# Batch 2's score products all raw in the prologue and tile 1, squares summed by adding DMAs, softmax chain in a fixed order

## The chip, the cores and the metric

The kernel runs on one core of one Trainium2 chip. The metric is the device time of one execution in microseconds; for the kernel before it is the median of two runs.

## The reference

Four batches of a channel attention, then a feed-forward layer on its output:

```python
B, N, C = (4, 6080, 256)
qn = q / (np.linalg.norm(q, axis=1, keepdims=True) + 1e-06)
kn = k / (np.linalg.norm(k, axis=1, keepdims=True) + 1e-06)
s = kn.transpose(0, 2, 1) @ qn / tau
a = softmax(s)                        # over the last axis, 256 x 256 a batch
x = (v @ a).reshape(B * N, C)         # 24320 x 256
h = x @ w_in                          # 256 x 2048
out = np.maximum(0.01 * h, h) @ w_out # 2048 x 256
```

The softmax line stands for four lines of the reference (maximum off, exponential, sum, division). The scores need, besides the product of k and q over 6080 rows, the sum of squares of each column of q and of k.

## The kernel before, in words

**Tiles and windows.** The output is made in 24 tiles (6 a batch, `NT`), each of 1024 rows (the last of a batch 960), in two halves. A tile has 8 windows (`NPAIR`), one for each pair of 128-wide slices of the 2048 hidden channels, twice over; so a batch has 48 windows (`WPB`). The loop at L854 to L894 issues one window after another. In a window, seven `block_product` calls (L546) of three matmuls each form a Strassen-like product of a split `v` and the combined weights `w_split`; ACT copies the sums (`taken`, L574), DVE adds (`add`, L569), ACT applies the leaky function and casts, DVE forms the low part (`leaky`, L557). The matmuls with `w_out` (`ffn_out`, L583) of the window before are dealt out between them by `out(n)`, 24 a window. All float32 values of these products are kept as a high and a low part in float32r, and a product takes three passes.

**Weights of a batch.** The combined weights are `w_in` multiplied by the batch's turned softmax matrix `aT`: `w_product` (L395) on PE, `w_taken` (L409) on ACT, `w_parts` (L417) on DVE, which gives six steps for each of four `j`: two of sums (L430, L431), then for each of two pairs `begin` (three blocks split) and `rest` (four blocks). For batch 1, `w_parts` writes straight into `w_split` tiles (`w_tile`, L390: 4 buffers) that the windows of tile 1 use; for `j` 1 to 3 it runs inside tile 1 (`w_early`, L698). From tile 2 on, `w_load` (L481) fetches them from DRAM.

**Scores.** Class `Scores` (L110). The 6080 rows are 48 chunks of 128 (one with 64 rows), in 24 groups of `G` = 2. `load` (L124) fetches a group of q and k with two DMAs from SP. `product(j)` (L168) multiplies a chunk either raw, as float32 (two calls), or, where `cast` (ACT, L157) and `low` (DVE, L162) have made a split tile, in six float32r calls. `square` (ACT, L151) and `add_square` (DVE, L154) sum the squares of a chunk. Then comes the softmax chain: `sums`, `norms_mm` (PE), `norms_taken`, `norms_begun`, `norms` (DVE), `rows_mm` (PE), `rows_taken`, `scaled` (DVE), `exps` (ACT), `normed` (DVE), `turn` (PE), `turned_high` (ACT), `turned_low` (DVE).

**The prologue** (L767 to L842) does batch 1's 24 groups raw (squares in whole groups, added by DVE at L142), its softmax chain, the split of tile 1's `v` (`v_parts`, L520, eleven steps on DVE), the first `w_product` and `w_parts`, and between them `FILL` = 5 groups, 10 chunks, of batch 2, raw. The order of instructions on an engine is chosen there by the framework's scheduler, by the order of the program and its own estimates, save where `tc.issue_after` sets a lower limit. Raw groups of batch 2, conversion blocks and weights share the tag `raw` (4 buffers).

**Conversions.** `w_in` and `w_out` arrive as 64-bit floats; `f64_split` (L320) turns a block into two parts with work on DVE and ACT. Four of 16 blocks are done in the prologue's first part, 12 in windows 0 to 5, two a window (`convert`, L741).

**What sets the order in the windows.** `in_order(engine)` (L99) chains an instruction to the last one issued on its engine, so the order of the windows' own work is written out by hand. Background work stands in queues (`todo`, L615); `put(queue, length, fn, then)` (L630) adds an entry with a planned length, and `slot(queue, room)` (L621) at fixed places of a window takes entries from the head of that queue while they fit in the room. `at(w, fn)` (L618) sets the window in which an entry is put. Batch 2's remaining 38 chunks are put by `chunk_work` (L652) in windows 8 to 33 (L752 to L758): cast and square on ACT, low part and add on DVE, the six matmuls in the next window. Its softmax chain is put from window 34 on (`norm_work`, `row_work`, `turn_work`, L664 to L677), and the weights for tile 7 (`w_work`, L679) from window 39. Batches 3 and 4 do all 48 chunks split.

SP issues all DMAs, in one queue, POOL a memset for the short chunk of each batch.

## Time and profile before

| | |
|---|---|
| median of 2 runs | 2224.7 us (2224.56 to 2224.85) |
| span of the profiled execution, first to last instruction | 2225.9 us |
| mean granted clock of TensorE | 0.990 |
| busy PE / weight load | 2174.0 us / 1814.1 us |
| busy DVE / ACT / POOL | 1488.5 us / 1483.2 us / 2.8 us |
| DMA | 324.74 MB, mean 146 GB/s |

PE is TensorE's matmul, PEld its weight load, DVE VectorE, ACT ScalarE, POOL GpSimd, SP SyncE. The profiled execution's span lies 1.2 us above the median of the runs. Times in views are microseconds from the start of the span, unless ns is written; a wait is written as the waiting instruction, an arrow, and what released it, with the total, the number of waits and the longest. The granted clock is the share of full speed that the throttle let through. L12 is line 12 of the kernel. The end of a matmul is modelled; the distance from one start to the next is what shows its cost.

### The profile page before, as it was taken

What the parts mean: (1) busy time and instruction counts of PE and PEld (TensorE: products, weight loads), DVE (VectorE), ACT (ScalarE), POOL (GpSimd) and SP (SyncE); (2) the same over time, 40 slices, a digit from 0 to 9 for tenths busy, and PEclk for the clock granted to TensorE, in tenths of its full rate; (3) what the DMA queues carried; (4) which work ended last, traced back from release to release, by engine and by line L of the source; (5) the groups of instructions that cost most, each with busy time, mean ns of one, the idle gap of its engine ahead of it and who ended that gap; (6) DMA issues with size and microseconds to landing.
All of it is one profiled execution on the core that took longest, in us unless ns stands there. A gap on an engine that the chain in (4) does not pass through costs nothing.

```text
span 2225.9 us, 27253 instructions
## 1 busy us (share of the span) xinstructions
PE 2174.0 (98%) x9940; PEld 1814.1 (81%) x9940; DVE 1488.5 (67%) x2651; ACT 1483.2 (67%) x2563; POOL 2.8 (0%) x10
## 2 busy tenths in 40 slices
PE   9679999999999999999999999999999999999999
PEld 7467888888888888888887888888888888888887
DVE  7986667666766776666766667676677655556554
ACT  6556777766657777776656777777665666666665
POOL 0000000000000000000000000000000000000000
PEclk9889999999999999999999999999999999999999
DMA  9435343342753434433464344343354432332331
GB/s 347 145 142 200 121 155 134 130 157 83 241 204 112 156 123 145 154 116 138 147 227 156 119 159 159 115 155 129 121 192 156 146 137 83 138 121 100 119 118 36
DMA packets 98967, 324.74 MB, mean 146 GB/s; under 512 B 10257, under 2 KB 22033, under 8 KB 98833
## 3 DMA queue, kind: packets, MB, share of 16 engines
q1 hardware_dynamic: 98832, 323.00, 42.1%
q8 instruction: 78, 1.28, 0.2%
q14 instruction: 57, 0.46, 0.1%
HBM read 264.50 MB, written 58.46 MB: 145 GB/s over the span
## 4 chain that ended last, share of the span: by engine, by line
PE 89%; DVE 5%; DMA 3%; ACT 2%; issue 0%; SPq 0%; ACTq 0%; DVEq 0%
PE ps_o L597 44%; PE ps_x L551 22%; PE ps_z L551 11%; PE ps_y L551 5%; PE ps_s L182 5%; PE ps_s L401 1%; DMA qk_raw<-in_k_dram 1%; DVE h L572 1%; DVE g_split L565 1%; DMA w_dram<-w_rest 1%; ACT h L562 1%; ACT g_split L563 1%; DMA f_raw<-in_w_out_dram 1%; DMA qk_raw<-in_q_dram 1%; DVE v_split L516 0%
## 5 line engine op out<-in xcount | busy, mean ns | idle before, releaser
L597 PE MATMUL ps_o<-g_split,w_out_split 128*128 128x512 f32 (+1 forms) x4608 | 1165.5, 388 | 0.0
L597 PEld LDWEIGHTS ps_o<-g_split,w_out_split 128*128 128x128 f32 x4608 | 867.7, 188 | 175.5
L565 DVE TENSOR_TENSOR g_split<-h,g_split 128x512 fp32r<-128x512 f32 (+1 forms) x768 | 525.0, 684 | 395.3 <-ACT g_split L563 394.4
L551 PE MATMUL ps_x<-v_split,w_split 128*128 128x512 f32 (+1 forms) x2304 | 653.7, 392 | 29.4 <-DVE w_split L439 16.2
L562 ACT ACTIVATE h<-h 128x512 f32<-128x512 f32 (+1 forms) x576 | 361.8, 628 | 292.3 <-DVE h L572 292.3
L578 ACT COPY h<-ps_x 128x512 f32<-128x512 f32 (+1 forms) x576 | 334.3, 580 | 312.4 <-PE ps_x L551 311.7
L551 PEld LDWEIGHTS ps_x<-v_split,w_split 128*128 128x128 f32 x2304 | 423.7, 189 | 114.0 <-ACT h L578 12.4
L563 ACT CAST g_split<-h 128x512 fp32r<-128x512 f32 (+1 forms) x768 | 473.4, 616 | 23.9
L572 DVE TENSOR_TENSOR h<-ps_z,h 128x512 f32<-128x512 f32 (+1 forms) x384 | 262.0, 682 | 284.7 <-ACT h L578 278.0
L551 PE MATMUL ps_z<-v_split,w_split 128*128 128x512 f32 (+1 forms) x1152 | 324.4, 390 | 6.3 <-DVE h L572 6.3
L551 PEld LDWEIGHTS ps_z<-v_split,w_split 128*128 128x128 f32 x1152 | 216.5, 188 | 52.5 <-DVE h L572 8.1
L551 PE MATMUL ps_y<-v_split,w_split 128*128 128x512 f32 (+1 forms) x576 | 162.9, 391 | 0.6 <-ACT w_a L411 0.6
L572 DVE TENSOR_TENSOR h<-ps_y,h 128x512 f32<-128x512 f32 (+1 forms) x192 | 131.3, 684 | 0.6
L551 PEld LDWEIGHTS ps_y<-v_split,w_split 128*128 128x128 f32 x576 | 109.0, 190 | 23.5 <-ACT w_a L411 1.1
L182 PEld LDWEIGHTS ps_s<-qk_split 128*128 128x128 f32 x804 | 114.1, 190 | 11.3 <-issue 1.0
L562 ACT ACTIVATE h<-ps_x 128x512 f32<-128x512 f32 (+1 forms) x192 | 112.8, 587 | 10.8 <-PE ps_x L551 10.8
L182 PE MATMUL ps_s<-qk_split 128*128 128x256 f32 x804 | 118.1, 283 | 0.0
L160 ACT CAST qk_split<-qk_raw 128x512 fp32r<-128x512 f32 x134 | 82.9, 619 | 31.8 <-PE ps_s L182 24.0
L516 DVE TENSOR_TENSOR v_split<-v_raw,v_split 128x512 fp32r<-128x512 f32 (+1 forms) x144 | 98.7, 686 | 4.7
L155 DVE TENSOR_TENSOR sq_acc<-sq_acc,sq 128x512 f32<-128x512 f32 x141 | 96.2, 683 | 0.0
L164 DVE TENSOR_TENSOR qk_split<-qk_raw,qk_split 128x512 fp32r<-128x512 f32 x134 | 91.6, 684 | 2.3 <-ACT qk_split L160 2.3
L152 ACT ACTIVATE sq<-qk_raw 128x512 f32<-128x512 f32 x141 | 88.8, 633 | 2.0 <-DMA qk_raw<-in_k_dram 2.0
(101 smaller groups left out, 726.7 us busy)
## 6 DMA issues: line engine op xcount, KB each, us to landing
w_split<-w_dram SPq DMA_DIRECT2D x184, 896.0 KB, 4.7
qk_raw<-in_q_dram SPq DMA_DIRECT2D x92, 256.0 KB, 3.6
qk_raw<-in_k_dram SPq DMA_DIRECT2D x92, 256.0 KB, 3.8
v_raw<-in_vT_dram SPq DMA_DIRECT2D x40, 512.0 KB, 4.9
out_dram<-o_sb SPq DMA_DIRECT2D x80, 256.0 KB, 4.2
win<-win_dram SPq DMA_DIRECT2D x24, 512.0 KB, 4.1
w_dram<-w_rest SPq DMA_DIRECT2D x24, 512.0 KB, 3.1
w_dram<-w_first SPq DMA_DIRECT2D x24, 384.0 KB, 3.4
```

The lines of the kernel that those rows point to most:

```text
L152: return nc.scalar.activation(out=out, in_=self.chunk(j), func=AF.Square)
L155: return nc.vector.tensor_tensor(out=self.acc[0], in0=self.acc[0], in1=sq, op=ALU.add)
L164: return nc.vector.tensor_tensor(out=sp[:, :, 1, :], in0=self.chunk(j), in1=f32(sp[:, :, 0, :]), op=ALU.subtract)
L182: mm = nc.tensor.matmul(out=s, lhsT=lhsT, rhs=rhs, start=False, stop=last and n == len(passes) - 1, skip_group_check=True,)
L516: last = nc.vector.tensor_tensor(out=sp[:, 1, 0:w], in0=src, in1=f32(sp[:, 0, 0:w]), op=ALU.subtract)
L551: mm = nc.tensor.matmul(out=ps[:, 0:n], lhsT=w[:, x, a, :], rhs=sp[:, y, 0:n], start=first and k == 0, stop=k == 2, skip_group_check=True,)
L562: nc.scalar.activation(out=out[:, 0:n], in_=h[:, 0:n], func=AF.Prelu, alpha=0.01)
L563: issued["act"] = nc.scalar.copy(out=sp[:, 0, 0:n], in_=out[:, 0:n])
L565: issued["dve"] = nc.vector.tensor_tensor(out=sp[:, 1, 0:n], in0=out[:, 0:n], in1=f32(sp[:, 0, 0:n]), op=ALU.subtract)
L572: issued["dve"] = nc.vector.tensor_tensor(out=h[:, 0:n], in0=ps[:, 0:n], in1=h[:, 0:n], op=ALU.add)
L578: issued["act"] = nc.scalar.copy(out=h[:, 0:n], in_=ps[:, 0:n])
L597: issued["pe"] = nc.tensor.matmul(out=o_ps[i][j][h][:, 0:n], lhsT=wo[x][:, f, h * P:(h + 1) * P], rhs=sp[:, y, 0:n], start=p == 0 and earl ...
```

## The change

- The prologue multiplies 8 groups (16 chunks) of batch 2 raw instead of 5, loaded into buffers of `g_split` (groups 0 to 4) and `w_split` (groups 5 to 7) by `spare`. The engines' order from `sums` on is written out by `run`, which chains each step to the one before it on its engine; steps of `v_parts` stand between those of the chain, and the weight steps are issued in the order 2, 0, 1, 3, then three of `v`, then 4, 5.
- The other 16 groups are put raw into windows 0 to 7, two a window (`group_work`): four entries in queue `pe`, squares of a whole group in `act`. Their raw tiles use the tag `qk_split` (3 buffers); a group is loaded for at the window before its own.
- Squares: group 0's go straight into the accumulator (a tile in the buffer of `w_rest`), each other group's are written over its raw tile, and a DMA from POOL adds that tile into the accumulator. `fold` adds the two halves on DVE after the last. The tile of raw data is free when its adding DMA is done.
- Batch 2's softmax chain starts at window 12 instead of 34, its steps 4 windows apart instead of 2; the weights for tile 7 start at window 21 instead of 39.
- The high part of tile 1's `v` is copied by ACT, and in tile 1 one slot of ACT has room for 2.2 instead of 1.8.

The diff (left out: `sums` now returns its last instruction):

```diff
--- before.py
+++ after.py
@@ -21,7 +21,7 @@
 AHEAD = 8
 EARLY_LOAD = (12, 14, 16, 18)
 EARLY_SPLIT = (17, 19, 21, 23)
-FILL = 5
+FILL = 8
 VBUFS = 10
 GBUFS = 5
 RBUFS = 4
@@ -143,6 +143,20 @@
 
         def first_squares(self, i):
             nc.scalar.activation(out=self.acc[i], in_=self.raw[i], func=AF.Square)
+
+        def group_product_squares(self, i):
+
+            raw = self.raw[i]
+            if i == 0:
+                return nc.scalar.activation(out=self.acc[0], in_=raw, func=AF.Square)
+            ins = nc.scalar.activation(out=raw, in_=raw, func=AF.Square)
+            nc.gpsimd.dma_start(out=self.acc[0], in_=raw, accum_op=ALU.add)
+            return ins
+
+        def fold(self, acc):
+            both = self.acc[0]
+            self.acc = [acc]
+            return nc.vector.tensor_tensor(out=acc, in0=both[:, :, 0, :], in1=both[:, :, 1, :], op=ALU.add)
 
         def chunk(self, j):
             i, x = self.of[j]
...
@@ -512,7 +529,7 @@
     def v_split_of(i, name, src):
         w = widths[i % NT]
         sp = work.tile([P, 2, TW], F32R, name="v_split", tag="v_split", bufs=VBUFS)
-        nc.vector.tensor_copy(out=sp[:, 0, 0:w], in_=src)
+        (nc.scalar.copy if i == 0 else nc.vector.tensor_copy)(out=sp[:, 0, 0:w], in_=src)
         last = nc.vector.tensor_tensor(out=sp[:, 1, 0:w], in0=src, in1=f32(sp[:, 0, 0:w]), op=ALU.subtract)
         v_split[i, name] = sp
         return last
@@ -661,6 +678,13 @@
             sq = temp(name="sq").rearrange("p (x c) -> p x c", x=2)
             put("act", 0.6, lambda: sc.square(j, sq), [("dve", 0.7, lambda: sc.add_square(sq))])
 
+    def group_work(sc, i):
+
+        a, b = sc.groups[i]
+        put("pe", 0.5, lambda: sc.product(a))
+        then = [("dve", 0.7, lambda: sc.fold(acc_tile()))] if i == len(sc.groups) - 1 else []
+        put("pe", 0.5, lambda: sc.product(b), [("act", 1.05, lambda: sc.group_product_squares(i), then)])
+
     def norm_work(sc):
         put("pe_late", 1, sc.norms_mm, [
             ("dve", 0.5, sc.norms_taken, [("dve", 1.8, sc.norms_begun, [("dve", 2.0, sc.norms)], True)], True),
@@ -749,19 +773,27 @@
     for b in range(1, B):
         w0 = (b - 1) * WPB
         sc = scores[b]
-        done = FILL * G if b == 1 else 0
-        begin_at, span = (NPAIR, 25) if b == 1 else (2, 31)
-        when = {j: w0 + begin_at + (j - done) * span // (NCHUNK - done) for j in range(done, NCHUNK)}
-        for i in range(done // G, len(sc.groups)):
-            at(max(w0, when[i * G] - 3), lambda sc=sc, i=i: sc.load(i, qk_raw()))
-        for j in range(done, NCHUNK):
-            at(when[j], chunk_work, sc, j)
-        e = w0 + begin_at + span + 1
+        if b == 1:
+            per = -(-(len(sc.groups) - FILL) // NPAIR)
+            for i in range(FILL, len(sc.groups)):
+                w = w0 + (i - FILL) // per
+                at(max(w0, w - 1), lambda sc=sc, i=i: sc.load(i, work.tile([P, 2, G, C], F32, name="qk_raw1", tag="qk_split", bufs=3)))
+                at(w, group_work, sc, i)
+            e = w0 + NPAIR + 4
+        else:
+            begin_at, span = 2, 31
+            when = {j: w0 + begin_at + j * span // NCHUNK for j in range(NCHUNK)}
+            for i in range(len(sc.groups)):
+                at(max(w0, when[i * G] - 3), lambda sc=sc, i=i: sc.load(i, qk_raw()))
+            for j in range(NCHUNK):
+                at(when[j], chunk_work, sc, j)
+            e = w0 + begin_at + span + 1
+        apart = 4 if b == 1 else 2
         at(e, norm_work, sc)
-        at(e + 2, row_work, sc)
-        at(e + 4, turn_work, sc)
-        at(e + 1, win_load, 0)
-        at(e + 5, w_work, b, 0)
+        at(e + apart, row_work, sc)
+        at(e + 2 * apart, turn_work, sc)
+        at(e + 2 * apart - 3, win_load, 0)
+        at(e + 2 * apart + 1, w_work, b, 0)
 
 
     sc, nxt = scores[0], scores[1]
@@ -794,52 +826,70 @@
             sc.product(j)
         if i in EARLY_SPLIT:
             conv.split()
-    sc.sums()
-    sc.norms_mm()
-    sc.norms_taken()
-    sc.norms_begun()
-    after["dve"] = sc.norms()
+
+    def run(engine, fn, *args):
+        with in_order(engine):
+            issued[engine] = ins = fn(*args)
+        return ins
+
+    def spare(i):
+        if i < GBUFS:
+            return work.tile([P, 2, G, C], F32, name="qk_raw1", tag="g_split", bufs=GBUFS)
+        t = work.tile([P, 2, NS, P], F32, name="qk_raw1", tag="w_split", bufs=4)
+        return t.rearrange("p x s f -> p (x s f)")[:, 0:2 * G * C].rearrange("p (x g c) -> p x g c", x=2, g=G)
+
+    nxt.begin([work.tile([P, 2, G, C], F32, name="sq_acc1", tag="w_rest", bufs=1)], bank("s"))
+
+    def fill(n):
+        for i in range(n, n + 1):
+            for j in nxt.groups[i]:
+                run("pe", nxt.product, j)
+            run("act", nxt.group_product_squares, i)
+
     with tc.issue_after(after["load"].ins):
-        for i in range(min(2, FILL)):
-            nxt.load(i, qk_raw())
-    sc.rows_mm()
-    sc.rows_taken()
-    after["scaled"] = sc.scaled()
-    sc.exps()
-    after["normed"] = sc.normed()
-    nxt.begin([acc_tile()], bank("s"))
-    filled = []
-
-    def fill(n):
-        for i in range(len(filled), min(len(filled) + n, FILL)):
-            for j in nxt.groups[i]:
-                nxt.product(j)
-                if j == 0:
-                    nxt.square(j, nxt.acc[0])
-                else:
-                    sq = temp(name="sq").rearrange("p (x c) -> p x c", x=2)
-                    nxt.square(j, sq)
-                    nxt.add_square(sq)
-            if i + 2 < FILL:
-                nxt.load(i + 2, qk_raw())
-            filled.append(i)
-
-    with tc.issue_after(after["dve"].ins):
-        fill(2)
-    sc.turn("x")
-    sc.turned_high()
-    after["turned"] = sc.turned_low()
-    with tc.issue_after(after["scaled"].ins):
-        fill(1)
-        for _, fn in v_parts(0):
-            fn()
+        for i in range(FILL):
+            nxt.load(i, spare(i))
+    v_tile = [fn for _, fn in v_parts(0)]
+
+    def v_do(n):
+        for fn in v_tile[:n]:
+            run("dve", fn)
+        del v_tile[:n]
+
+    fill(0)
+    run("dve", sc.sums)
+    run("pe", sc.norms_mm)
+    fill(1)
+    fill(2)
+    run("dve", sc.norms_taken)
+    run("dve", sc.norms_begun)
+    run("dve", sc.norms)
+    run("pe", sc.rows_mm)
+    fill(3)
+    fill(4)
+    v_do(1)
+    run("dve", sc.rows_taken)
+    run("dve", sc.scaled)
+    run("act", sc.exps)
+    fill(5)
+    v_do(2)
+    run("dve", sc.normed)
+    run("pe", sc.turn, "x")
+    fill(6)
+    run("act", sc.turned_high)
+    v_do(2)
+    run("dve", sc.turned_low)
     for h in range(CH):
-        w_product(0, 0, h, "yz"[h])
-        w_taken(0, 0, h)
-    for _, fn in w_parts(0, 0):
-        fn()
-    with tc.issue_after(after["turned"].ins):
-        fill(FILL)
+        run("pe", w_product, 0, 0, h, "yz"[h])
+        run("act", w_taken, 0, 0, h)
+    fill(7)
+    v_do(3)
+    order = list(w_parts(0, 0))
+    for x in (2, 0, 1, 3):
+        run("dve", order[x][1])
+    v_do(3)
+    for x in (4, 5):
+        run("dve", order[x][1])
 
     outs = []
 
@@ -872,7 +922,7 @@
             slot("dve", 2.2)
             block_product(i, p, x, S2, "T2", False, False)
             h12 = taken(i, x)
-            slot("act", 1.8)
+            slot("act", 1.8 if i else 2.2)
             block_product(i, p, z, S1, "T1", True, False)
             out(5)
             slot("pe", 1)
```

More of the change, by code (lines that the diff above doesn't have):

```diff
@@ L192, in sums @@
             nc.vector.tensor_tensor(out=acc, in0=acc, in1=other, op=ALU.add)
-            nc.vector.tensor_tensor(out=acc[:, :, 0, :], in0=acc[:, :, 0, :], in1=acc[:, :, 1, :], op=ALU.add)
+            last = nc.vector.tensor_tensor(
+                out=acc[:, :, 0, :], in0=acc[:, :, 0, :], in1=acc[:, :, 1, :], op=ALU.add
+            )
             self.acc = [acc[:, :, 0, :]]
+            return last
         def norms_mm(self):
```

## The prediction

> **What bounds the kernel now.** I read the page of the profile first, then a table of busy times by stretch, cut where the windows of tile 1 begin, then who waited for whom on PE.
>
> ```profile
> span 2225.9 us, 27253 instructions
> PE 2174.0 (98%) x9940; PEld 1814.1 (81%) x9940; DVE 1488.5 (67%) x2651; ACT 1483.2 (67%) x2563; POOL 2.8 (0%) x10
> PE   9679999999999999999999999999999999999999
> ```
>
> PE is the bound from the fourth slice on. Only the second and third slices have room on it.
>
> ```profile
> 48.70:77.50 28.80, 17.72 (x71) 13.47 (x71) 26.91 (x67) 12.65 (x25) 0.00 (x0) 0.86 0.54 191
> 77.50:92.70 15.20, 10.78 (x28) 7.09 (x28) 12.90 (x33) 5.44 (x10) 0.00 (x0) 0.59 0.50 190
> 92.70:112.70 20.00, 12.75 (x51) 9.26 (x52) 17.22 (x35) 14.84 (x26) 0.00 (x0) 0.94 0.36 121
> 112.70:127.30 14.60, 14.13 (x51) 10.89 (x52) 12.52 (x32) 7.33 (x14) 0.00 (x0) 0.85 0.44 177
> 127.30:146.10 18.80, 12.32 (x52) 9.23 (x50) 13.80 (x28) 12.61 (x22) 0.00 (x0) 0.96 0.32 112
> 146.10:164.90 18.80, 15.54 (x52) 11.90 (x52) 16.58 (x38) 8.37 (x15) 0.00 (x0) 0.77 0.41 155
> 164.90:180.20 15.30, 12.41 (x53) 9.30 (x51) 11.27 (x23) 10.15 (x18) 0.00 (x0) 1.00 0.47 134
> 180.20:192.20 12.00, 10.69 (x46) 8.42 (x47) 7.87 (x22) 5.65 (x10) 0.00 (x0) 1.00 0.83 319
> 192.20:202.40 10.20, 10.20 (x47) 8.45 (x46) 8.73 (x16) 6.48 (x12) 0.00 (x0) 1.00 0.25 89
> 202.40:500.00 297.60, 297.60 (x1418) 250.38 (x1417) 202.78 (x327) 216.64 (x376) 0.00 (x0) 1.00 0.42 145
> ```
>
> The columns are the stretch, its length, the busy time of PE, weight load, DVE, ACT and POOL, the granted clock, the DMA share and GB/s. The first row is the softmax chain of batch 1, the next eight are windows 0 to 7 (tile 1), the last is windows 8 to about 34, in which batch 2's other 38 chunks are multiplied. Three readings. In the last row PE is busy 297.6 of 297.6 us: work taken off PE there shortens the run one for one. Tile 1 takes 124.9 us, and PE is busy in 98.8 of them, some at a clock of 0.59 to 0.85: there is room, 26.1 us and more. Window 7, with neither conversions nor new weights, takes 10.2 us, all PE.
>
> ```profile
> PE ps_x L551 <- DVE w_split L439: 16.2, 4, 5.3
> PE ps_x L551 <- ACT h L578: 7.2, 7, 1.9
> PE ps_x L551 <- DVE w_split L440: 5.0, 3, 3.0
> ```
>
> In tile 1, PE waits above all for the next pair's weights from DVE, four times and up to 5.3 us. DVE is busy 12.5 to 17.2 us in windows 1 to 4, near the whole length: tile 1 is a chain through DVE.
>
> **Term 1, products taken out of windows 8 to 34.** What a chunk costs on PE, split and raw, is read from starts.
>
> ```profile
> 49.63 3.62 PE L182 MATMUL ps_s<-qk_raw 128*128 128x256 f32 x16
> 53.09 0.95 PE L200 MATMUL ps_y<-ones,sq_acc 128*128 128x1 f32 x8
> ...
> 77.47 0.77 PE L551 MATMUL ps_x<-v_split,w_split 128*128 128x512 f32 x1 [3.93 <-DVE w_split L439]
> ...
> 215.08 0.88 PE L182 MATMUL ps_s<-qk_split 128*128 128x256 f32 x6
> 215.79 0.86 PE L551 MATMUL ps_x<-v_split,w_split 128*128 128x512 f32 x3
> L182 PE MATMUL ps_s<-qk_split x228: 277/283/283, 215.1 to 490.3; 128*128 128x256 f32 x114
> ```
>
> (The last row is the group of split products in windows 8 to 34.) A split chunk takes 215.79 - 215.08 = 0.71 us; the group's 228 matmuls are 38 chunks of 6. All 38 leave a stretch where PE is full: 38 x 0.71 = **-27.0 us**. The ACT squares and casts and DVE adds and low parts that go with them lay beside that full PE and bring nothing there (cover: PE's 297.6 us). A raw chunk takes 4 recorded matmuls; 16 of them go from 49.63 to 53.09, 3.46 us, so 0.865 us a chunk: raw is dearer on PE by 0.155 us. The 32 chunks put into tile 1 are 27.7 us of PE there; the 6 further ones in the prologue 5.2 us.
>
> **Term 2, the softmax chain.** Rows of DVE's timeline, then ACT's, then the DVE group of the adds that go.
>
> ```profile
> 64.34 0.16 DVE L285 TENSOR_SCALAR den<-den 128x2 f32<-128x2 f32 x1
> 66.34 0.61 DVE L288 TENSOR_SCALAR s_sb<-s_sb,den 128x256 f32<-128x256 f32 x2
> 70.68 0.68 DVE L309 TENSOR_TENSOR aT<-ps_x,aT 128x512 fp32r<-128x512 f32 x1
> 77.10 0.36 DVE L439 CAST w_split<-w_a 128x128 fp32r<-128x128 f32 x2
> ```
>
> ```profile
> 67.95 0.58 ACT L306 CAST aT<-ps_x 128x512 fp32r<-128x512 f32 x1
> 73.59 0.59 ACT L411 COPY w_a<-ps_z 128x512 f32<-128x512 f32 x1
> ```
>
> ```profile
> L155 DVE TENSOR_TENSOR sq_acc<-sq_acc,sq 128x512 f32<-128x512 f32 x9 | 6.2, 684 | 0.0
> L141 ACT ACTIVATE sq<-qk_raw 128x1024 f32<-128x1024 f32 x22 | 23.1, 1054 | 5.5 <-DMA qk_raw<-in_k_dram 5.3
> ```
>
> DVE is busy 26.9 of 28.8 us here, and the chain stands behind other DVE work three times: the normalising waits from 64.50 to 66.34 (1.8 us), the low part of the turned matrix from 68.53 to 70.68 (2.2), the first weights from 74.18 to 77.10 (2.9). A fixed order can give at most these 7 us. Nine adds leave DVE (6.2 us), one v copy goes to ACT. Against it, on PE 16 chunks instead of 10 stand in a fixed order between the steps, and on ACT two squares (2 x 1.05 us) stand ahead of the exponentials and one ahead of the cast of the turned matrix. I give back 3 of the 7: **-4 us**. Bounds: -7 (nothing given back) and +5 (no gain, and the 5.2 us of extra products all on the chain).
>
> **Term 3, 32 raw chunks in tile 1.** Lower bound: each stretch is as long as before or as PE's work, whichever is more, with 4 chunks (3.46 us) a window. Window 0: 10.8 + 3.5 is under 15.2. Windows 1 and 2: 26.9 + 6.9 = 33.8, under 34.6. 3 and 4: 27.9 + 6.9 = 34.8, under 37.6. 5 and 6: 23.1 + 6.9 = 30.0 over 27.3, +2.7. Window 7: +3.5. Sum +6.2. Upper bound: all 27.7, for the products stand ahead of the new pair's weight product in PE's queue, so weights, wait and next window could all move back by their length. Between: in windows 1 and 3 I lose half (3.5 of 6.9), since DVE works off conversions meanwhile, in 0, 2 and 4 a third (3.3 of 10.4), in 5 to 7 the 6.2: **+13 us**. ACT's 16 squares (16.9 us) fit: ACT is busy 70.9 of 124.9 us, and they stand where PE has over 4 us of products before it needs ACT again (T1, 5 out products, two raw chunks, T3).
>
> **Term 4, the adding DMAs.** None exists in this trace: POOL has 10 instructions. Nearest rows (KB each, median us from issue to landing):
>
> ```profile
> qk_raw<-in_k_dram SPq DMA_DIRECT2D x92, 256.0 KB, 3.8
> v_raw<-in_vT_dram SPq DMA_DIRECT2D x40, 512.0 KB, 4.9
> w_dram<-w_rest SPq DMA_DIRECT2D x24, 512.0 KB, 3.1
> qk_raw<-in_q_dram SPq DMA_DIRECT2D x4, 64.0 KB, 2.2
> ```
>
> An add moves 512 KB but reads two operands. Below: one pass, 3.1 us. Above: two of the slowest passes, 9.8 us. From the rows: fixed part 2.2, one pass 3.1 - 2.2 = 0.9, two passes 1.8, with about 0.5 for the issue: T = 4.5 us, nearest to the 512 KB rows. The 23 adds go into one accumulator, so each waits for the last one: they are a chain. It starts when group 1 is squared: norms product 53.09, end about 53.9, products 1.73, square 1.05, say 57. Two places wait for it. (a) Groups 5 to 7 of the prologue lie in three of the four weight buffers; the second pair's weights (the fifth weight step on DVE) need the buffer of group 5, so add 5 done: 57 + 5T. In the new order that step comes at about 80 (weights from 73, then 3.8 of weight steps and 3.3 of v). Queued behind it on DVE: the first adds and low parts of window 0, and for those waits PE. (b) In tile 1 the raw groups share three buffers: group 11 needs group 8's, so add 8 done and a load (3.8): 57 + 8T + 3.8, wanted at about 95 in window 1. Its load waits at the head of SP's queue:
>
> ```profile
> 137.97 9.82 SPq L317 DMA_DIRECT2D f_raw<-in_w_out_dram x4
> ```
>
> behind it there stand loads of raw weights like these, the weight stores and v. At T = 4.5, (a) is 79.5, in time, and (b) 96.8, late by 1.8: **+2 us**. Later groups have 16 to 17 us a pair against 9. The fold on DVE in window 8 waits for the last add, but PE has its last blocks and out products meanwhile: 0. At T = 3.1 the term is 0; at 6.5 it is 9.5 + 8.3 = 17.8; at 9.8 it is 26 + 18, and with 19.6 us a pair against 17 some 14 more, 58.
>
> The Trainium skill (SBUF — State Buffer, Who interferes with whom) speaks against the change: a DMA issued from GpSimd has its descriptors written by GpSimd, which is locked out while VectorE runs a copy, cast or scalar operation in a two-port mode; its example goes from about 620 to 3100 ns. By it an add here would be an estimated 2.5 us longer, 7 us, and the kernel would come out a few us slower than before; by the row above (POOL all but unused) no run here shows it yet, though DVE is 86 to 93% busy in the prologue, windows 1 and 4.
>
> **Sum.** -27 - 4 + 13 + 2 = -16 us. The span is 2225.9 us, 1.2 above the median of 2224.7; the difference taken off the median gives 2208.7, **2209 us**.
>
> **Rivals.**
> *The adds are slow.* Without term 4 the change is worth 18 us, so from T = 6.5 it is lost and from there the kernel is slower. At T = 8: (a) 17, (b) 12.8, together 30, so +12, 2237. At 9.8: +40, 2265. For: no row shows a second operand, other traffic holds the DMA engines at shares of 0.32 to 0.83, and it is one chain. Against: 512 KB passes take 3.1 us, and over tile 1 the chain needs far less than is there.
> *Nothing overlaps.* Term 3 is 27.7: -27 - 4 + 27.7 + 2 = -1.3, 2223. For: the waits for weights end in DVE work that begins after the weight product. Against: PE is idle at other places too (7.2 us for ACT).
> *All overlaps.* Terms 2 and 3 at their good ends, no wait for adds: -27 - 7 + 6.2 = -27.8, 2197. For: slow clocks in tile 1 go away with idle PE. Against: DVE is the chain there and is not relieved.
> *The order isn't what it says:* the fixed order lengthens the chain instead: +5 in term 2, -7 in all, 2218.
>
> **How the numbers follow.** Chances: forecast 0.40 (own range 2201 to 2217), slow adds 0.22, nothing overlaps 0.15, all overlaps 0.18, order costs 0.05. From 2193 to 2240 I leave out half of the slow adds and a little below 2197. 2% is 44 us, about what a measurement of this kernel can tell from no change: a gain of 44 has no term that could bring it (0.02); a loss of 44 needs adds at or above 9.8 us (0.05); within, 0.93.
>
> **What would show it.** Windows 8 to 34 without score products, each 10.2 us and full. Window 0's first product about 4 us earlier. Tile 1 about 138 us instead of 124.9, the granted clock there nearer 1. Adds on a queue of POOL's, some 4.5 us apart while they queue. Wrong: adds of 6.5 us or more, a DVE wait of several us at L439 in window 0, PE waiting for a raw load in window 1, conversions late behind SP, or tile 1 over 150 us.

## The result and the profile after

The changed kernel takes **2262.1 us** (median of 2 runs, 2259.89 to 2264.29) against 2224.7: 37.4 us longer, ratio 1.017 (95% 1.014 to 1.0199). The forecast of 2209 us has the wrong sign, and the time lies 22 us above the upper end of its range. The rival of the slow adds gives such a time for adds between 8 us (2237) and 9.8 us (2265); whether its mechanism is the right one is the question of the experiments.

First the page of the changed kernel: its span, PE's busy time, and PE and the DMA engines in 40 slices.

```profile
span 2258.1 us, 27056 instructions
PE 2180.1 (97%) x9864; PEld 1816.0 (80%) x9864; DVE 1436.8 (64%) x2560; ACT 1463.8 (65%) x2508; POOL 22.9 (1%) x33
PE   7687699999999999999999999999999999999999
DMA  9777723554324434344276343343354432332331
```

PE now has room in five slices instead of two, up to about 280 us, and just there the DMA engines are busy at 0.7 and more.

The table of busy times by stretch, cut as before where a window's first product begins: windows 0 and 1, then 6 to 9, then what follows. The columns are the stretch, its length, PE, weight load, DVE, ACT and POOL busy, granted clock, DMA share, GB/s.

```profile
88.50:110.70 22.20, 12.54 (x46) 9.66 (x44) 10.95 (x29) 6.73 (x11) 2.69 (x3) 0.77 0.85 222
110.70:136.30 25.60, 16.22 (x69) 12.26 (x68) 17.18 (x34) 16.70 (x28) 2.59 (x3) 0.95 0.73 192
...
217.50:233.00 15.50, 15.50 (x61) 12.66 (x62) 7.83 (x22) 7.63 (x12) 0.86 (x1) 0.89 0.91 282
233.00:261.40 28.40, 16.61 (x62) 13.35 (x61) 8.81 (x16) 8.47 (x14) 2.59 (x3) 0.76 0.63 162
261.40:271.60 10.20, 10.20 (x46) 8.45 (x45) 3.65 (x6) 7.86 (x14) 0.86 (x1) 1.00 0.94 283
271.60:289.50 17.90, 12.14 (x46) 9.60 (x45) 7.40 (x12) 6.96 (x13) 0.00 (x0) 0.81 0.42 118
289.50:500.00 210.50, 210.36 (x934) 173.22 (x934) 138.02 (x273) 132.55 (x230) 0.52 (x1) 1.00 0.45 153
```

Three things are to be seen. Window 0's first product runs at 88.5, 11.0 us later than before (77.47), where the forecast had it 4 earlier. Tile 1 takes 172.9 us (88.5 to 261.4) instead of 124.9, where the forecast had 138; the worst window is the last, 28.4 us with 16.6 of PE work, and it has neither conversions nor new weights. And window 9, after the tile, takes 17.9 us for 12.1 of PE work, where the forecast put the wait of the fold at nothing. Behind that PE is full at a clock of 1.00, as forecast. Window 8 starts at 261.4 against 202.4 before: 59.0 us lost (11.0 and 48.0), and 7.7 more in window 9; what follows gives 34.5 back, which leaves the 32.2 us between the two spans.

Who PE waited for, in the whole run (total, times, longest):

```profile
PE ps_x L568 <- ACT h L595: 17.6, 3, 9.7
PE ps_s L196 <- DMA qk_raw<-in_k_dram: 16.9, 4, 11.8
...
PE ps_s L187 <- DMA qk_raw<-in_k_dram: 12.4, 1, 12.4
```

None of them names an adding DMA. The waits of PE name the last step only; one has to ask what that step waited for. The chain of work, followed back through tile 1, does it: 58.4% of the stretch from 88 to 292 us is `DMA sq_acc<-qk_raw`, the adds. Some of its pieces (start, length, what):

```profile
105.86 5.25 DMA sq_acc<-qk_raw
...
146.91 4.60 DMA sq_acc<-qk_raw
...
226.25 11.17 DMA sq_acc<-qk_raw
...
268.76 7.50 DMA sq_acc<-qk_raw
276.28 0.04 DVE sq_acc L159
```

The shortest of all its 23 adds takes 4.5 us, the longest 11.2. The three places where something waits for an add can be read from the timelines, DVE's and PE's here. An engine's idle time and its releaser stand in brackets.

```profile
100.22 0.43 DVE L456 CAST w_split<-w_a 128x128 fp32r<-128x128 f32 x2 [6.78 <-DMA sq_acc<-qk_raw]
276.28 0.69 DVE L159 TENSOR_TENSOR sq_acc<-sq_acc 128x512 f32<-128x512 f32 x1 [6.50 <-DMA sq_acc<-qk_raw]
```

```profile
61.96 2.04 PE L187 MATMUL ps_s<-qk_raw,zeros 128*128 128x512 f32 x2 [12.40 <-DMA qk_raw<-in_k_dram]
104.73 1.65 PE L568 MATMUL ps_x<-v_split,w_split 128*128 128x512 f32 x3 [9.65 <-ACT h L595]
205.79 3.35 PE L196 MATMUL ps_s<-qk_raw 128*128 128x256 f32 x8 [2.87 <-DMA qk_raw<-in_k_dram]
247.45 2.90 PE L196 MATMUL ps_s<-qk_raw 128*128 128x256 f32 x6 [11.79 <-DMA qk_raw<-in_k_dram]
280.03 1.65 PE L568 MATMUL ps_x<-v_split,w_split 128*128 128x512 f32 x3 [5.76 <-ACT h L595]
```

At 100.22 the first weight step of the second pair has waited 6.8 us for the add that still reads its buffer (the forecast's place (a)); the adds of window 0 stand behind it on DVE, so ACT's `h` is late and PE idle for 9.65 us. At 276.28 the fold has waited 6.5 us at the head of DVE's queue, and DVE's adds of window 9 stand behind it: PE idle for 5.76. At 247.45 PE waits for group 22's raw data, whose buffer group 19's add held until 237.4 (226.25 and 11.17); the load itself, beside the next add, takes the other 10 us. The wait at 61.96 has nothing to do with adds: group 0 of the prologue came late. SP's timeline tells why:

```profile
43.35 0.33 SPq L134 DMA_DIRECT2D qk_raw<-in_q_dram  x1
...
49.30 0.38 SPq L334 DMA_DIRECT2D f_raw<-in_w_out_dram  x1
...
52.70 0.48 SPq L129 DMA_DIRECT2D qk_raw<-in_q_dram  x1
...
55.89 0.34 SPq L134 DMA_DIRECT2D qk_raw<-in_k_dram  x1
```

The loads are issued in an order that the program didn't fix: groups 5 to 7 go out from 43.35 on, then conversion blocks (L334), and group 0, the one that the first product needs, only from 52.70 to 55.89 (L129 and L134). The page of the profile gives no order to look for; the line numbers and the start times do.

### The profile page after: what moved, and what is told of

It is laid out like the page before. It is cut to its first block, busy times and chain, and to the rows that moved or that the text cites. A ratio compares the mean times of both kernels' runs of the same rounds, so it can differ in the third digit from the quotient of the medians.

```text
span 2258.1 us, 27056 instructions
## 1 busy us (share of the span) xinstructions
PE 2180.1 (97%) x9864; PEld 1816.0 (80%) x9864; DVE 1436.8 (64%) x2560; ACT 1463.8 (65%) x2508; POOL 22.9 (1%) x33
## 3 DMA queue, kind: packets, MB, share of 16 engines
q1 hardware_dynamic: 98832, 323.00, 41.7%
## 4 chain that ended last, share of the span: by engine, by line
PE 85%; DMA 6%; issue 2%; DVE 1%; ACT 1%; POOLq 0%; SPq 0%; DVEq 0%
PE ps_o L614 43%; PE ps_x L568 21%; PE ps_z L568 11%; PE ps_y L568 5%; DMA sq_acc<-qk_raw 5%; PE ps_s L196 3%; PE ps_s L418 1%; DVE h L589 0%; ACT h L579 0%; ACT g_split L580 0%; DVE g_split L582 0%; DMA w_dram<-w_rest 0%; DMA qk_raw<-in_k_dram 0%; DVE v_split L533 0%; DVE w_rest L457 0%
## 5 line engine op out<-in xcount | busy, mean ns | idle before, releaser
L196 PEld LDWEIGHTS ps_s<-qk_split 128*128 128x128 f32 x576 | 81.7, 190 | 8.3 <-issue 1.0
L196 PE MATMUL ps_s<-qk_split 128*128 128x256 f32 x576 | 84.9, 283 | 0.0
L174 ACT CAST qk_split<-qk_raw 128x512 fp32r<-128x512 f32 x96 | 59.4, 619 | 25.9 <-PE ps_s L196 22.1
L178 DVE TENSOR_TENSOR qk_split<-qk_raw,qk_split 128x512 fp32r<-128x512 f32 x96 | 65.7, 684 | 2.3 <-ACT qk_split L174 2.3
L532 DVE CAST v_split<-v_raw 128x512 fp32r<-128x512 f32 (+1 forms) x138 | 57.4, 416 | 14.1 <-PE ps_x L568 14.1
L196 PE MATMUL ps_s<-qk_raw 128*128 128x256 f32 x192 | 50.1, 411 | 16.9 <-DMA qk_raw<-in_k_dram 16.9
```

The costliest lines, as they stand in the source:

```text
L174: return nc.scalar.copy(out=sp[:, :, 0, :], in_=self.chunk(j))
L178: return nc.vector.tensor_tensor(out=sp[:, :, 1, :], in0=self.chunk(j), in1=f32(sp[:, :, 0, :]), op=ALU.subtract)
L196: mm = nc.tensor.matmul(out=s, lhsT=lhsT, rhs=rhs, start=False, stop=last and n == len(passes) - 1, skip_group_check=True,)
L532: (nc.scalar.copy if i == 0 else nc.vector.tensor_copy)(out=sp[:, 0, 0:w], in_=src)
```

## The experiments

Each edit is against the changed kernel, and its time stands beside runs of the kernel before on the same chip (medians 2223.4 to 2224.7). The question that they share is which effect of the adds costs the time: that they are there at all (traffic), that they hold buffers, or that something stands behind them in a queue.

**Group 0 in time.** The prologue's eight loads are issued in the order 0 to 7, by chaining them, the conversion blocks and tile 1's raw loads on SP's queue (the last two are left out of the cut).

```diff
...
-            nxt.load(i, spare(i))
+            run("sp", nxt.load, i, spare(i))
```

> The changed kernel with one thing added: on SP the eight groups of the prologue are loaded in the order 0 to 7, and the conversion blocks and tile 1's raw groups only after them. Theory (most of the loss is waits for DMAs that were ordered behind others): PE's wait of 12.4 us for group 0 goes, the softmax chain starts about 12 us earlier, the waits for adds stay; 2262 - 12 = 2250 us. Rival (the DMA engines are simply full, at a share of 1.0, and what is loaded later is missed later): conversions come late instead, 2257 us or more.

Measured 2253.8 us, ratio 1.0137 (1.012 to 1.0154): 8.3 us less than the changed kernel. Window 0 starts at 78.6 instead of 88.5, but part of that is lost to the adds again, which begin earlier and stand among more loads. The adds' issues on POOL, and DVE's wait in window 0:

```profile
57.62 1.01 POOL L153 DMA_DIRECT2D sq_acc<-qk_raw  x1 [13.17 <-DMA win_dram<-win_early]
67.11 0.91 POOL L153 DMA_DIRECT2D sq_acc<-qk_raw  x1 [8.49 <-DMA sq_acc<-qk_raw]
76.19 0.86 POOL L153 DMA_DIRECT2D sq_acc<-qk_raw  x1 [8.17 <-DMA f_raw<-in_w_in_dram]
```

```profile
DVE w_split L457 <- DMA sq_acc<-qk_raw: 10.7, 1, 10.7
```

Now the chain starts at 57.6, as the forecast had it (57), and its first two adds take 9 us each; the wait at place (a) has grown from 6.8 to 10.7. The fold waits longer too: window 9 takes 23.1 us here, against 17.9. (The execution that was profiled took 2259.7 us, 5.8 above the median, so these waits are those of a long one.) So the late load of group 0 is a loss of its own, some 8 us with the adds as they are, and not the cause of the rest.

**Place (a) taken away.** As above, and the raw groups 0 to 2, whose adds come first, lie in the weight buffers instead of 5 to 7.

```diff
-        if i < GBUFS:
+        if i > 2:
```

> The one before, and besides the three weight buffers hold groups 0 to 2 of the prologue, the g_split buffers groups 3 to 7, so that the second pair's weights wait for no add later than the second. Theory: DVE's wait of 6.8 us at the weights and PE's of 9.7 us after it go too; 2240 us, 10 below the one before. Rival (window 0 is bound by DVE anyway, its wait only hides other work): within 3 us of the one before.

Measured 2261.6 us, ratio 1.0166 (1.0151 to 1.0181). The expectation failed by 22 us. The wait for the weight buffer is gone (window 0 takes 20.7 us instead of 27.3 in the run with the loads in order, by the starts of the first `ps_y` products), yet window 1 takes 37.5 instead of 26.0: PE waits 9.8 us there for a raw load. The adds are one chain, and a place that no longer waits for it lets the next place reach it sooner.

**The adds left out.** The 23 adding DMAs aren't issued, so the accumulator holds the squares of group 0 alone.

```diff
-            nc.gpsimd.dma_start(out=self.acc[0], in_=raw, accum_op=ALU.add)
```

> The changed kernel without the 23 adding DMAs: only group 0's squares reach the accumulator, so the norms of batch 2 are those of two chunks; all other work is there, and a raw buffer is free when its squares are made. Theory (adds hold buffers): the late group 0 (12.4 us) stays, the waits at the weights (9.7), at the raw loads of tile 1 (16.9) and at the fold (5.8) go, most of the excess of 41 us in windows 1 to 7 with them: 2262 - 32 = 2230 us, tile 1 at about 150 us. Rival (raw products in front of the weight product don't overlap, whatever the adds do): 2262 - 10 = 2252 us, tile 1 at 165 us or more.

Measured 2216.5 us, ratio 0.9964 (0.9951 to 0.9977). The adds cost 2262.1 - 2216.5 = 45.6 us, all of the loss and 8 more, and 13.5 more than the waits that the expectation had added up. Tile 1 in this run, with all its raw products and squares and no add:

```profile
91.30:226.70 135.40, 120.26 (x502) 97.33 (x501) 97.80 (x212) 85.30 (x137) 0.00 (x0) 0.94 0.56 196
```

135.4 us against 172.9, with 8.8 us less of PE's busy time for the same 502 matmul records (the clock is 0.94 instead of 0.87).

**The changed prologue alone.** Eight groups are multiplied in the prologue with their adds; the other 32 chunks are split and multiplied in windows 8 to 34 as in the kernel before, with the softmax chain of batch 2 at its old place and the fold in window 4.

```diff
-            per = -(-(len(sc.groups) - FILL) // NPAIR)
-            for i in range(FILL, len(sc.groups)):
...
+            for i in range(done // G, len(sc.groups)):
+                at(max(w0, when[i * G] - 3), lambda sc=sc, i=i: sc.load(i, qk_raw()))
+            for j in range(done, NCHUNK):
+                at(when[j], chunk_work, sc, j)
...
```

> The changed kernel's prologue (8 groups, adding DMAs, fixed order), but the other 32 chunks split in windows 8 to 33 and batch 2's chain at window 34, as before the change. Theory: what the prologue does alone is window 1 some 18 us late, and 6 chunks fewer later bring 4.3 us; 2225 + 18 - 4 = 2239 us. The other 23 us of the loss are tile 1's. Rival (all of it is the prologue's, tile 1 only inherits it): 2255 us or more.

Measured 2236.8 us, ratio 1.0058 (1.0041 to 1.0075). The prologue alone loses 12 us, although 6 split chunks go (6 x 0.71 = 4.3). Its window 0 starts at 89.52, 12.1 us later than before, and its tile 1 takes 126.6 us against 124.9; DVE waits only 1.1 us for a weight buffer here. So this loss is the late start: the late load of group 0 and a chain that gained little (term 2 below). Tile 1's part adds the other 25, net of the 32 split chunks that it takes away (32 x 0.71 = 22.7).

**The raw loads off SP's queue.** Tile 1's raw loads are issued from POOL, so that on SP nothing stands behind them.

```diff
...
-                last = nc.sync.dma_start(out=raw[:, x, x0:len(at), :], in_=rows[:, t0:t0 + len(at) - x0, :])
+                last = queue.dma_start(out=raw[:, x, x0:len(at), :], in_=rows[:, t0:t0 + len(at) - x0, :])
...
```

> The changed kernel with tile 1's raw groups loaded from POOL's queue instead of SP's: a load still waits for the add that frees its buffer, but what stands behind it on SP (conversion blocks, weight stores, weight loads) no longer does. Theory 1 (SP's queue, which stood 92 us at its head for adds, is the way in which the adds do harm): half of the 33 us that are left beside the late group 0 goes, 2245 us. Theory 2 (the raw buffers themselves come free too late): 2258 to 2264, as before. Theory 3 (the adds' traffic slows the other transfers): as before too.

Measured 2261.9 us, ratio 1.0177 (1.0161 to 1.0193): nothing gained. In the changed kernel the raw loads had held SP's queue for 92.1 us in all while they waited for adds; in this run no such wait is left on SP. PE waits for raw data longer than before, 23.6 us against 16.9. The run isn't a clean one, for the wait moved to POOL's queue: the loads stand there between the adds, and POOL waits 45.8 us in nine waits at the head of a load for an add. But what stands on SP behind the loads no longer waits for them, and that alone gains nothing. So the theory of SP's blocked queue falls as the whole cause.

**Traffic apart from holding.** The adds are all there, but read a constant tile of zeros, so they hold no raw tile and no weight buffer. Left out: the squares of groups 1 to 23; zeros are added in their place.

```diff
...
-            nc.gpsimd.dma_start(out=self.acc[0], in_=raw, accum_op=ALU.add)
+            nc.gpsimd.dma_start(out=self.acc[0], in_=self.nil, accum_op=ALU.add)
...
```

> The changed kernel with the 23 adding DMAs taking a tile of zeros as source instead of the squares (batch 2's norms are those of group 0 alone; one buffer fewer for temporaries makes room): the same traffic in the same chain, but no raw or weight buffer is held by an add and no add waits for ACT. Theory 3 (traffic): 2240 us or more. Theories 1 and 2 (holding): 2217 to 2222 us, as without the adds.

Measured 2223.0 us, ratio 0.9997 (0.9987 to 1.0006). The whole difference is in this pair of numbers: 23 adds as mere traffic cost 2223.0 - 2216.5 = 6.5 us, and that they stand between the squares and whatever waits for them costs 2262.1 - 2223.0 = **39.1 us**. In that second part are the buffers that they hold and the late end of the chain, for an add of zeros needn't wait for its squares either, and the last one is issued at 221.1 instead of 268.8. (Each run set against the kernel before beside it, the two parts are 7.6 and 37.8.) The same run gives the price of an add, for from the second on POOL never waits for data but only for the add before:

```profile
79.78 0.86 POOL L153 DMA_DIRECT2D sq_acc<-nil  x1 [3.98 <-DMA sq_acc<-nil]
84.62 0.86 POOL L153 DMA_DIRECT2D sq_acc<-nil  x1 [3.98 <-DMA sq_acc<-nil]
...
211.79 0.86 POOL L153 DMA_DIRECT2D sq_acc<-nil  x1 [9.98 <-DMA sq_acc<-nil]
221.10 1.08 POOL L153 DMA_DIRECT2D sq_acc<-nil  x1 [8.45 <-DMA sq_acc<-nil]
```

4.84 us where they come one behind the other in a calm stretch, up to 10.9 where raw loads and weights go at the same time, and (221.10 - 65.38) / 22 = 7.1 on the average from the first issue to the last.

**The fold out of the way.** The fold, which waits for the last add, is put into window 11 instead of right behind group 23's square.

```diff
-        then = [("dve", 0.7, lambda: sc.fold(acc_tile()))] if i == len(sc.groups) - 1 else []
+        then = []
...
+            at(e - 1, put, "dve", 0.7, lambda sc=sc: sc.fold(acc_tile()))
```

> The changed kernel with the fold put into DVE's queue in window 11 instead of behind the last squares. Theory (DVE stood 6.5 us for the last add, and PE 5.8 behind it): 2262 - 6 = 2256 us. Rival (the wait only hides another): 2260 to 2264.

Measured 2251.8 us, ratio 1.0128 (1.0115 to 1.0142): 10.3 us less. Windows 8, 9 and 10 take 10.2 us each again and PE is full in them:

```profile
260.50:291.10 30.60, 30.60 (x137) 25.34 (x135) 17.17 (x27) 21.24 (x37) 0.86 (x1) 1.00 0.65 190
```

This is the one edit that undoes a single wait and keeps its gain, for nothing in the windows behind it waits for the chain. (Expected were 6; the profiled executions differ by 9.8.)

**Earlier squares.** ACT's last slot in tile 1 gets room for a square, so that a pair's second group is squared in the window of its product and not in the next.

```diff
-            slot("act", 0.65)
+            slot("act", 0.65 if i else 1.7)
```

> The changed kernel with room for 1.7 instead of 0.65 in the last ACT slot of tile 1's windows: the second group of a window is squared in that window and no longer in the next, about 12 us sooner, and its add, and the load into its buffer, with it. Theory 2 (three raw buffers: a buffer's round trip of load, product, square, add sets the pace of tile 1, 21.6 us a window against 16.9 without adds): the trip of 42 us for three groups gets 12 us shorter, tile 1 loses 25 us, 2237 us. Rival (the chain of adds itself sets the pace, at 7.1 us an add beside other traffic; or the loads do): 2255 us or more.

Measured 2258.9 us, ratio 1.0164 (1.0149 to 1.018): 3.2 us instead of 25. The wait at the raw loads did go, as meant (PE's waits for them in tile 1 fall from 16.9 to 4.3 us), but there were others behind it. To see whether the fold had hidden the gain, both edits were put together:

> The last ScalarE slot of the raw groups stands at 1.7 in tile 1 and a pair's second group is squared in the same window as its first (as in the run with the early squares), and the fold and its ones-products stand in window 11 (as in the run with the late fold). Theory (the three raw buffers' round trip is what stretches windows 2 to 7, and the wait of the fold hid what the earlier squares saved there): the gains of both add up and a little more, since window 7 no longer hands its delay to the fold, 2239 us. Rival (the earlier squares only move the wait, and are worth the 3 us that they brought alone): 2249 us, the late fold's 10 us and 3 more.

Measured 2248.8 us, ratio 1.011 (1.0093 to 1.0128): the late fold's 10 us and 3 more, so the rival holds. The stretches tell why:

```profile
110.80:146.20 35.40, 18.49 (x68) 13.78 (x68) 18.82 (x37) 18.20 (x30) 3.44 (x4) 0.82 0.69 184
146.20:257.50 111.30, 97.09 (x390) 78.51 (x391) 69.61 (x149) 60.31 (x97) 9.60 (x11) 0.92 0.77 226
```

Windows 2 to 7 take 111.3 us instead of 125.1 (136.3 to 261.4 above): the 14 us are there. Window 1 takes 35.4 instead of 25.6 and gives 10 of them back. What it waits for is read from SP's queue and ACT's:

```profile
122.76 0.43 SPq L134 DMA_DIRECT2D qk_raw<-in_k_dram  x1
123.30 0.89 SPq L334 DMA_DIRECT2D f_raw<-in_w_out_dram  x2
```

```profile
132.49 0.65 ACT L346 ACTIVATE f_raw<-f_raw 128x512 f32<-128x512 uint32 x1 [12.69 <-DMA f_raw<-in_w_out_dram]
```

The conversion's loads stand on SP behind a raw load that waits for its buffer, that is for an add, and then take 9 us to land (ACT starts on the first at 132.49). ACT stands 12.7 us at the conversion, with the copy of `h` behind it that window 1 needs. This is the forecast's place (b) by its other branch, "conversions late behind SP".

**All four mended, adds kept.** The ordered loads, the swapped buffers, the earlier squares and the late fold together.

> The changed kernel, adding DMAs and all, with four remedies: loads in order, weight buffers for groups 0 to 2, the last ACT slot at 1.7, the fold in window 11. If the waits are what the adds cost, and the remedies add up: 2262 - 8 - 10 - 25 = 2219 us, near the 2223 of the chain with nothing held. If each remedy only uncovers the next wait: 2235 us or more.

Measured 2236.6 us, ratio 1.0065 (1.0049 to 1.008): 25.5 us better than the changed kernel, 12 worse than the kernel before, as the rival had it. The four edits are worth 8.3, -7.8 (on top of the first), 3.2 and 10.3, 14 in sum; together they bring 25.5. That fits a chain with several places that wait for it: part of what one edit frees, the next place takes, until that is mended too. Raw loads still make PE wait 12.8 us in this run (16.9 in the changed kernel).

**Term 2 alone.** The changed prologue with its loads in time and buffers swapped, no adds, the other chunks split as before. Left out: the squares of the 16 chunks of the prologue.

> The softmax chain's part alone: the prologue of the changed kernel with ordered and swapped loads and 16 raw chunks, no adding DMAs (the squares of these 16 chunks are left out of the norms), the other 32 chunks split in windows 8 to 33, batch 2's chain at window 34. My prediction's term 2 (the chain starts tile 1 earlier by 4 us and it stays): 2224 - 4 - 4 = 2216 us. Rival (window 0 starts some 11 us earlier, but the conversions that DVE then hasn't done come back in windows 0 and 1, so that tile 1 ends as before): 2224 - 4 = 2220 us.

Measured 2216.5 us, ratio 0.997 (0.9959 to 0.9981). Without adds and squares, the prologue starts window 0 much earlier, in PE's timeline:

```profile
69.78 1.05 PE L569 MATMUL ps_x<-v_split,w_split 128*128 128x512 f32 x3
```

Before, it stands at 77.47, so the chain gains 7.7 us. Window 0 gives 3.6 of them back (18.8 us to the next window's first product at 88.59, against 15.2 to 92.69 before), and window 8 starts at 198.05 instead of 202.39: 4.3 us. The run says less of term 2 than it seems, for the squares that it leaves out stand on ACT between the steps of the chain. ACT's cast of the turned matrix in this run, and below it in the run with all four remedies, whose loads come in the same order and which has the squares (and the adds):

```profile
63.95 0.58 ACT L323 CAST aT<-ps_x 128x512 fp32r<-128x512 f32 x1 [2.43 <-PE ps_x L314]
```

```profile
69.44 0.56 ACT L323 CAST aT<-ps_x 128x512 fp32r<-128x512 f32 x1
```

Window 0 starts at 76.24 there, only 1.2 us earlier than before, and at 78.56 in the run with the loads in order.

**The squares without adds.** From these a version follows that keeps the 48 raw products and needs no adding DMA: in windows 8 to 32, where ACT has room beside the full PE, each group is loaded a second time and squared, and DVE adds it, so that prologue and tile 1 are without squares; the softmax chain keeps its late place (window 34). Loads in order, buffers swapped.

```diff
...
+            for i in range(len(sc.groups)):
+                w = w0 + NPAIR + i
+                at(w - 2, lambda sc=sc, i=i: sc.load(i, qk_raw()))
+                at(w, group_square, sc, i)
+            e = w0 + NPAIR + 26
...
```

> All products of batch 2 raw as in the changed kernel, with the ordered and swapped loads of the prologue, but no squares there and no adding DMAs: batch 2's 24 groups are loaded a second time in windows 6 to 31, squared by ACT and added by DVE in windows 8 to 32, the chain from window 34 as before the change. Theory (the products' part of the change is worth 27 us, tile 1 loses 14 of them, the prologue nothing when its loads are in time; ACT and DVE have room beside PE from window 8 on): 2217 - 12 = 2205 us. Rival (the second load and the squares are not hidden, or the prologue still loses): 2215 us or more.

Measured **2208.3 us** (5 runs, 2206.6 to 2208.4), ratio 0.993 (0.9918 to 0.9943): faster than both kernels, 15.2 us under the median of 2223.4 of the kernel before beside it. The second load of some 12 MB costs nothing that can be seen in those windows, for PE stays full. Its windows 8 to 33, and below them the same 26 windows of the kernel before:

```profile
218.40:483.60 265.20, 265.20 (x1171) 219.59 (x1170) 180.46 (x268) 194.86 (x319) 0.00 (x0) 1.00 0.50 169
```

```profile
203.10:496.40 293.30, 293.30 (x1400) 246.81 (x1399) 199.62 (x320) 213.46 (x371) 0.00 (x0) 1.00 0.42 145
```

## Why the prediction was wrong, by its own steps

**What bounds the kernel now: right.** Where PE is full, work taken off it shortens the run one for one: 293.3 - 265.2 = 28.1 us for the 38 split chunks.

**Term 1, -27.0: right,** -28.1 in the two rows above.

**Term 2, -4: also wrong, though by less.** The 4.3 us at window 8 in the run of the chain alone are worth no more than an upper bound, for that run has none of the squares against which the forecast set a part of its 3 us. From group 0's first product to window 0's first product it takes 21.1 us, against 28.8 before (48.70 to 77.47). With the squares it takes 29.5 us in the run without adds (61.76 to 91.26), 26.5 in the changed kernel, 26.3 with adds that read zeros and 27.2 with all four remedies. So they give back most of the gain or all of it: at most 2.5 us are left, and the adds aren't the reason, since the longest of these runs has none. In the changed kernel another 12.4 us of waiting stand before that, because group 0's load stands on SP behind groups 5 to 7 and conversion blocks. That step was missing from the working: it costed the waits of the engines and left out the order of the prologue's loads, of which the change issues eight groups behind a single instruction. It costs about 8 us, by the run with the loads in order.

**Term 3, +13: about right.** Without adds, tile 1 takes 135.4 us against the forecast 138, 10.5 more than before. With group 0 in time the price is higher: 148.1 us in the run with reloaded squares (windows from 69.6 to 217.7), against 128.3 with the same prologue and no raw products in tile 1 (69.78 to 198.05), 19.8. Both lie between the bounds of 6.2 and 27.7.

**Term 4, +2: this is the step that failed; it measured 45.6.** Four of its sentences were wrong:

1. "T = 4.5 us, nearest to the 512 KB rows." In a calm stretch an add takes 4.84 to 5.1 us, so the estimate was fair there. Over the whole of tile 1 the mean is 7.1 (the run that only adds zeros) and single ones take 11. The nearest rows were medians over a run most of which has DMA shares of 0.3 to 0.4; the adds go where the share is 0.6 to 0.9. The adds also lengthen what goes beside them (with adds that read zeros the first two medians below are 6.5 and 6.6). KB each and median us to landing, without the adds and in the changed kernel:

```profile
f_raw<-in_w_out_dram SPq DMA_DIRECT2D x8, 512.0 KB, 4.1
w_dram<-w_split SPq DMA_DIRECT2D x8, 896.0 KB, 3.7
```

```profile
sq_acc<-qk_raw POOLq DMA_DIRECT2D x23, 512.0 KB, 5.7
f_raw<-in_w_out_dram SPq DMA_DIRECT2D x8, 512.0 KB, 7.0
w_dram<-w_split SPq DMA_DIRECT2D x8, 896.0 KB, 6.4
```

2. "Later groups have 16 to 17 us a pair against 9." This compared the rate of the adds with that of the products and left out the round trip: a raw tile is loaded, multiplied, squared (up to a window later, where ACT's slot has room), added, and only then free. With three tiles, group 22's product can't come before group 19's tile has gone once round: 205.79 to 247.45 in the changed kernel, 41.7 us for three groups, one of the longest trips. From group 8's product (90.08) to group 23's (254.46) three groups take 32.9 us on the average, 21.9 a pair against the 16 to 17 there are. The mean add of 7.1 is under the 8 to 8.5 a group, so the rate alone fits; the trip doesn't. The earlier squares, which shorten the trip, bring windows 2 to 7 from 125.1 to 109.6 us.

3. "The fold on DVE in window 8 waits for the last add, but PE has its last blocks and out products meanwhile: 0." It cost 10.3 us. The cover was named rightly for PE, but the wait is at the head of DVE's queue, and behind the fold there stand DVE's adds of the next blocks. What is queued behind the waiting instruction was asked for places (a) and (b) and not for this one.

4. Place (a) "in time" at 79.5: its working was right with the wrong T. The chain starts at 70.5 (group 0 late), four adds stand 5.05 to 6.3 us apart, and the fifth, issued at 91.98, ends when the weight step runs, at 100.22.

**The rivals.** The slow adds came nearest in size (2265 at 9.8 us), but the adds don't take 9.8 us on the average; the mean T is 7.1, for which the text's own formula gives (a) 57 + 35.5 - 80 = 12.5 and (b) 57 + 56.8 + 3.8 - 95 - 12.5 = 10.1, so -18 + 22.6 = +5 us, 2229. The rest is the trip through three tiles, the fold and group 0. *Nothing overlaps* and *all overlaps* don't decide, since without adds the kernel takes 2216.5 us. *The order isn't what it says* doesn't hold as it was meant, for the fixed order doesn't lengthen the chain (26.5 us against 28.8 above); what changed for the worse was the order of the loads, which the working left out.

**The rule that was weighed.** The Trainium skill (SBUF — State Buffer, Who interferes with whom) has GpSimd's descriptor writing locked out by VectorE's copies, casts and scalar operations in a two-port mode, by which the text estimated 7 us an add. The mean agrees and the cause isn't borne out by the rows. Two stretches of the changed kernel:

```profile
76.80:92.00 15.20, 10.73 (x47) 8.49 (x48) 14.80 (x35) 10.43 (x18) 2.59 (x4) 1.00 0.55 103
212.70:237.90 25.20, 21.24 (x86) 16.80 (x84) 15.20 (x37) 13.18 (x21) 1.72 (x2) 0.93 0.89 269
```

In the first DVE is busy 97% of the time and the three adds come 5.05 to 5.1 us apart; in the second DVE is busy 60%, the DMA share is 0.89, and the two adds take 8.7 and 11.2 us. In these two stretches the adds are long where the DMA engines are busiest, not where DVE is. No run isolates the instructions of VectorE that lock GpSimd out, so the rule itself stays untested.

**What stays open.** How the 39.1 us divide between the weight buffers, the three raw tiles, SP's queue and the fold can't be given as a sum of the edits, since their gains don't add up. Where they arise can be read from the starts of the windows. Windows 0 and 1, 2 to 7, and 8 and 9 in the run with adds that read zeros:

```profile
89.80:125.27 35.47, 25.89 (x112) 20.48 (x111) 27.90 (x63) 23.27 (x38) 4.90 (x6) 0.99 0.95 268
125.27:232.64 107.37, 96.04 (x390) 78.03 (x391) 70.84 (x153) 61.91 (x100) 11.47 (x13) 0.92 0.87 252
232.64:253.04 20.40, 20.40 (x91) 16.89 (x90) 11.00 (x18) 14.76 (x26) 0.00 (x0) 1.00 0.55 190
```

In the changed kernel they take 47.8, 125.1 and 28.1 us: 12.3, 17.7 and 7.7 more. Whether four or five raw tiles would have mended the trip wasn't tried. And the changed kernel gives back 6 us more behind the tile than the split chunks explain (34.5 against 28.1). About half of that seems to belong to the profiled execution of the kernel before, for against it the run of the chain alone, too, gives back 7.5 us from window 8 on, where only 6 split chunks (4.3 us) have gone; the rest no run tells.

## What to carry to other kernels

Where a transfer both reads a tile and is the last to let it go, cost the whole trip of the tile (load, use, square, add, load) over the number of tiles, not the rate of the transfers; and take the transfer's duration from a stretch as busy as the one it is put into. For each instruction that waits, ask what stands behind it on its engine or queue, for a cheap fold as much as for a load: in a chain with several such places, what one remedy frees can be lost at the next. And when loads are no longer tied to steps, read the order in which the queue issues them, for the one needed first may go out last.

## What the runs showed of the hardware

- An adding DMA of 512 KB from one SBUF tile into another takes 4.84 to 5.1 us from one to the next in a calm stretch, 7.1 on the average of tile 1 and up to 11.2 at a DMA share of 0.9; issuing it takes POOL 0.86 us.
- As pure traffic 23 of them cost a kernel whose DMA engines are at 0.6 to 0.9 only 6.5 us in 2220 (7.6 against the kernel before beside each run); they lengthen the transfers beside them (a store of 896 KB from 3.7 to 6.4 us, median).
- In tile 1 the same 502 matmul records are busy 120.3 us at a granted clock of 0.94 (without adds) and 129.0 us at 0.87, in the run in which PE waits longer. That the waiting lowers the clock isn't isolated by a run.
